# The last layer of an attention and expert kernel: blocks of 512 tokens, and each hidden chunk added at once to the running sums of its block

## The chip, the cores and the metric

The kernel runs on one core of one Trainium2 chip. The metric is the device time of one launch, in microseconds (us): the median over the runs shown. The core has five engines that work side by side, each in the order of its own queue: TensorE (PE, matrix products and transposes), VectorE (DVE), ScalarE (ACT), GpSimd (POOL) and SyncE (SP, which here only issues transfers).

## The reference

Three stages follow one another. Attention over 4 batches, 8 heads and 576 positions gives 2304 token rows of 512 numbers. A layer of 8 experts follows, two for each token. The last layer, the only one that the change touches, is a dense one:

```python
def _moe2_ref(x, w_in, w_out, alpha):      # x: 2304 x 512
    h = x @ w_in                           # w_in: 512 x 2048
    g = np.maximum(h, 0.0) + alpha * np.minimum(h, 0.0)
    return (g @ w_out).astype(np.float32)  # w_out: 2048 x 512
```

Its input x is, for each token, the weighted sum of two rows that the experts left in memory.

## The kernel before

Precision is kept by splitting every float32 operand into a high part and a remainder (float32r); each product is then three matrix products: high by high, remainder by high, high by remainder. `w_hi` (L170, ACT) and `w_lo` (L173, POOL or DVE) split a weight of 128 x 1024, which `w_load` (L165 or L167, SP) brought into a ring of two raw buffers in `m_v0`. Weights 64 to 71 are w_in, 72 to 79 are w_out. 72 to 74 are split during the experts; 75 to 79 are split in the first block of the last layer, after the chunks f = 1, 3, 5, 7 and 9.

The 2304 tokens are 18 tiles of 128. Before, the last layer goes over 9 blocks of 256 tokens (2 tiles). In each block there are two phases.

- **Up.** For each of 16 chunks f of 128 hidden channels, `mm1` (L197) issues 12 products: the stationary operand is 128 x 128 of w_in, the moving one 256 tokens of x, the result one tile of `psum_t` (three buffers). DVE takes it out in two steps (L944, L945) into `tmp`, ACT writes the high part h (L947), POOL the remainder (L948). The hidden values of the whole block stay in `hh` and `hl`.
- **Down.** For each of the 2 tiles, `mm2` (L215) issues 48 products: stationary 128 hidden channels by 128 tokens, moving 128 x 512 of w_out, all summed in one bank of `psum_s`. ACT then copies the sum to one of two `y_tile` buffers (L966) and SP writes it out (L968).

The next block's input is made meanwhile. `y_load` (L865, POOL) issues two indirect gathers for a tile; `combine` (L872 on ACT, L873 on DVE) makes their weighted sum; `x_split` turns it with four PE transposes (L186), and ACT (L189) and DVE (L190) write the two parts of X. Here y_load stands after the chunks 6 and 10 of the up phase, combine and x_split between the products of the down phase.

Nothing is reordered by a planner: each engine runs its instructions in the order in which the program writes them (`tc.manual_schedule()`), and waits on semaphores where an operand or a buffer is not ready.

Ahead of the last layer, expert blocks of 256 and 384 tokens use the same `mm1` and `mm2`. Behind it stands a loop that is run zero times unless an expert overflows.

Of the kernel before, what the change touches and what calls it, by code (L numbers as in the profile page):

```python
# [5 lines left out]
FR = mybir.dt.float32r  # L6
# [4 lines left out]
OP = mybir.AluOpType  # L11
# [3 lines left out]
HP = H // 2  # L15
# [4 lines left out]
NT = N // 128  # L20
# [13 lines left out]
def emit(tc, qt, kt, v, tau, wg, wn, noise, w1, w2, w_in, w_out, alpha, out):  # L34
# [3 lines left out]
    pe, dve, act, pool, sp = nc.tensor, nc.vector, nc.scalar, nc.gpsimd, nc.sync  # L38

    def f32(ap):  # L40
        return ap.bitcast(FT)

    with (
# [7 lines left out]
        yg = dp.tile([N + E * CAP, DM], FT, name="yg")  # L51
# [4 lines left out]
        def cut(t, o, shape, dt=FT):  # L56
            n = 1
            for d in shape:
                n *= d
            w = n * mybir.dt.size(dt) // 4  # L60
            ap = t[:, o:o + w]
            if dt != t.dtype:
                ap = ap.bitcast(dt)
            if len(shape) == 2:
                ap = ap.rearrange("p (a b) -> p a b", a=shape[0])
            if len(shape) == 3:
                ap = ap.rearrange("p (a b c) -> p a b c", a=shape[0], b=shape[1])
            return ap
# [30 lines left out]
        def psum_s():  # L99
            return pp.tile([128, 2, 512], FT, name="ps_s", tag="s", bufs=2)  # L100

        def psum_t(dt=FT):
            return pp.tile([128, 512], dt, name="ps_t", tag="t", bufs=3)
# [10 lines left out]
        alpha_t = cp.tile([128, F2 // 128], FT, name="alpha_t")  # L114
# [27 lines left out]
        WH, WL = {}, {}  # L142
# [11 lines left out]
        rows = [c0([DM]) for _ in range(2)] + [cut(m_rows, DM * i, [DM]) for i in range(2)]  # L154
        row_tile = Ring(rows)
# [13 lines left out]
        def w_hi(n):  # L169
            act.copy(WH[n], wraw[n])  # L170
# [10 lines left out]
            sp.dma_start(r, xg[e * N + t * 128:e * N + t * 128 + 128])  # L181

        def x_split(src, j, x):
            ps = (psum_v, psum_t, psum_t)[j]()
            for c in range(HP):
                pe.transpose(ps[:, c * 128:c * 128 + 128], src[:, c * 128:c * 128 + 128], ident)  # L186
            pv_ = ps.rearrange("p (c t) -> p c t", c=HP)
            xh = x[0][:, :, j * 128:j * 128 + 128]
            act.copy(xh, pv_)  # L189
            dve.tensor_tensor(x[1][:, :, j * 128:j * 128 + 128], pv_, f32(xh), op=OP.subtract)  # L190

        def mm1(ps, n, wc, x, col):

            k = 0
            for d in range(HP):
                for w, xx in ((WH, 0), (WH, 1), (WL, 0)):
                    pe.matmul(ps[:, :n], w[wc[d]][:, col:col + 128], x[xx][:, d, :n],  # L197
                              start=(k == 0), stop=(k == 11))
                    k += 1
            return ps[:, :n]  # L200

        def psum_1(f):
            return psum_t()
# [6 lines left out]
        def mm2(ps, t, n, fs, nf, wc, hs):  # L210
            for f in fs:
                o = f * n + t * 128
                w, c = wc[f // 2], (f % 2) * 512
                for k, (a, ww) in enumerate(((hs[0], WH), (hs[1], WH), (hs[0], WL))):
                    pe.matmul(ps, a[:, o:o + 128], ww[w][:, c:c + 512],  # L215
                              start=(f == 0 and k == 0), stop=(f == nf - 1 and k == 2))

        y_tile = []
# [428 lines left out]
        for b in range(1, B):  # L647
            o = 20 * b
# [31 lines left out]
        for n in range(W0):  # L680
            i = 66 + 2 * n
# [35 lines left out]
        for i in range(END):  # L717
# [29 lines left out]
            if outs:  # L747
                pv(iv)
                if units[iv][2] == HP - 1 or iv < SOLO:
                    T = group_evac(iv)  # L750
# [23 lines left out]
        tmp_tile = Ring([ct([512]) for _ in range(4)])  # L774
        raw64 = ct([1024])
# [9 lines left out]
        hh = mem.tile([128, 16 * 256], FR, name="m_hh")  # L785
        hl = mem.tile([128, 16 * 256], FR, name="m_gate")
        m_x = mem.tile([128, 3072], FR, name="m_v1")
        X = (cut(m_x, 0, [HP, 384], FR), cut(m_x, 1536, [HP, 384], FR))
# [58 lines left out]
        for n in range(W0, 72):  # L847
            t = 1 + 3 * (n - W0)
# [11 lines left out]
        yrows = {}  # L860

        def y_load(T, src):
            for k in range(2):
                r = row_tile()
                pool.indirect_dma_start(  # L865
                    out=r, out_offset=None, in_=src,
                    in_offset=bass.IndirectOffsetOnAxis(ap=posi[:, T, k:k + 1], axis=0))
                yrows[T, k] = r

        def combine(T):  # L870
            y0, y1 = yrows[T, 0], yrows[T, 1]
            act.activation(y0, y0, AF.Copy, scale=wts[:, T, 0:1])  # L872
            dve.scalar_tensor_tensor(y1, y1, wts[:, T, 1:2], y0, op0=OP.mult, op1=OP.add)  # L873

        near = yg[0:N + E * BLOCK0]
        bt = BLOCK0 // 128
        blocks = [(0, bt), (bt, CAP // 128)]
        HS = (hh, hl)
# [21 lines left out]
        for e in range(E):  # L900
            wc = [8 * e + d for d in range(4)]
            wc2 = [8 * e + 4 + d for d in range(4)]
            for bi, (t0, t1) in enumerate(blocks):
                if (e, bi) == (0, 0):
                    continue
                n = (t1 - t0) * 128
# [13 lines left out]
                for t in range(t1 - t0):  # L920
                    ps = psum_s()[:, 0]
                    for f in range(0, 8, 2):
                        mm2(ps, t, n, [f, f + 1], 8, wc2, HS)
                        if f % 4 == 0 and left and (t > 0 or not last):
                            j = left.pop(0)
# [7 lines left out]
            tick()  # L933


        nb = NT // 2
        tmp_tile.aps += [raw64[:, :512], raw64[:, 512:]]
        for j in range(nb):
            for f in range(16):
                hf, fo = divmod(f, 8)  # L940
                ps = mm1(psum_1(f), 256, [64 + 4 * hf + d for d in range(4)], X, fo * 128)
                tmp = tmp_tile()
                t_, g_ = tmp[:, :256], tmp[:, 256:]
                dve.tensor_scalar(t_, ps, 0.0, alpha_t[:, f:f + 1], op0=OP.min, op1=OP.mult)  # L944
                dve.scalar_tensor_tensor(g_, ps, 0.0, t_, op0=OP.max, op1=OP.add)  # L945
                h = hh[:, f * 256:f * 256 + 256]
                act.copy(h, g_)  # L947
                pool.tensor_tensor(hl[:, f * 256:f * 256 + 256], g_, f32(h), op=OP.subtract)  # L948
                if j == 0 and f in (1, 3, 5, 7, 9):
                    w = 75 + f // 2  # L950
                    w_hi(w)
                    w_lo(w, pool)
                    if w < 78:
                        w_load(w + 2)
                if j + 1 < nb and f in (6, 10):
                    y_load(2 * j + 2 + (f - 6) // 4, yg[:, :])
            for t in range(2):
                ps = psum_s()[:, 0]
                if j + 1 < nb:
                    combine(2 * j + 2 + t)  # L960
                mm2(ps, t, 256, range(6), 16, [72 + c for c in range(8)], HS)
                if j + 1 < nb:
                    x_split(yrows[2 * j + 2 + t, 1], t, X)
                mm2(ps, t, 256, range(6, 16), 16, [72 + c for c in range(8)], HS)
                y = y_tile[0]()
                act.copy(y, ps)  # L966
                r = (2 * j + t) * 128
                sp.dma_start(out[r:r + 128], y)  # L968

# [35 lines left out]
        with tc.For_i(0, rv, 1) as it:  # L1007
# [5 lines left out]
            for e in range(E):  # L1013
                ph = up(gx, [8 * e + d for d in range(4)])
                h = []
                for f in range(2):
                    g = gt()
# [12 lines left out]
            for hf in range(2):  # L1030
                ph = up(gx, [64 + 4 * hf + d for d in range(4)])
                for f in range(2):
                    g, h, t_ = gt(), gt(), gt()
                    act.copy(g, ph[:, f])
                    ps = turn(g)
                    for c in range(4):
                        a = 8 * hf + 4 * f + c
                        o = slice(c * 128, c * 128 + 128)
                        dve.tensor_scalar(t_[:, o], ps[:, o], 0.0, alpha_t[:, a:a + 1], op0=OP.min, op1=OP.mult)
                        dve.scalar_tensor_tensor(h[:, o], ps[:, o], 0.0, t_[:, o], op0=OP.max, op1=OP.add)  # L1040
                    for c in range(2):
                        n = 4 * hf + 2 * f + c
# [35 lines left out]
```

## Time and profile before

| what | us |
|---|---|
| median of 3 runs | 1221.8 |
| the runs | 1216.07, 1222.15, 1221.8 |
| the profiled execution, its own time | 1216.61 |
| its span, first to last instruction | 1214.8 |
| last layer: first product to end of the last product's time on the chain | 792.01 to 1203.34 |
| TensorE busy in the span | 1177.5 (97%) |
| VectorE, ScalarE, GpSimd busy | 603.6, 548.9, 519.8 |

The span is what the profile shows of one execution; its own time is 1.8 us longer. Two of the three runs are some 6 us above the third and above the profiled one. Times of rows are counted from the span's start.

### The profile page before, as it was taken

Reading aid. Unit: us, or ns where it says so; the run is one execution under the profiler, and the core shown is the slowest. Engines: PE = TensorE matmul, PEld = TensorE weight load, DVE = VectorE, ACT = ScalarE, POOL = GpSimd, SP = SyncE. Lnnn points to the kernel's source line nnn. Section 1 sums busy time; section 2 is a strip of 40 time slices with the busy share of each in tenths; the row PEclk is TensorE's granted clock in tenths of the full one; section 3 lists DMA queues with packets and bytes.
Section 4 is the critical chain, followed back from the end, with each engine's and each line's share of the span. In section 5 each row is a group of like instructions: output and inputs, shape, how many; then the busy total and the mean of one; then the engine's idle time right before and its main releaser. Section 6 shows DMA issues by size and latency. Waiting matters only on the chain.

```text
span 1214.8 us, 21729 instructions
## 1 busy us (share of the span) xinstructions
PE 1177.5 (97%) x8422; PEld 1046.1 (86%) x8422; DVE 603.6 (50%) x1413; ACT 548.9 (45%) x1109; POOL 519.8 (43%) x617
## 2 busy tenths in 40 slices
PE   7999989999889999999999999999999999999996
PEld 6887777877778989898989898998898898898895
DVE  7968888699534334334445333453352352352340
ACT  7977878778424444444444444441221221221220
POOL 6735545443234444435444444473351351351330
PEclk9999999999999999999999999999999999999998
DMA  7423222232235654556555555521110110110100
GB/s 216 127 83 128 77 91 79 88 114 88 105 147 165 208 191 160 172 205 201 181 175 167 204 183 187 186 96 36 44 44 18 45 44 19 44 45 18 44 10 19
DMA packets 60603, 135.27 MB, mean 111 GB/s; under 512 B 9680, under 2 KB 10320, under 8 KB 60496
## 3 DMA queue, kind: packets, MB, share of 16 engines
q1 hardware_dynamic: 54448, 114.61, 28.5%
q0 software_dynamic: 5760, 18.88, 4.6%
q8 instruction: 68, 1.11, 0.4%
q14 instruction: 39, 0.32, 0.1%
q10 hardware_dynamic: 288, 0.34, 0.1%
HBM read 93.96 MB, written 39.85 MB: 110 GB/s over the span
## 4 chain that ended last, share of the span: by engine, by line
PE 89%; DVE 6%; ACT 2%; issue 1%; DMA 1%; POOL 1%; DVEq 0%; POOLq 0%; ACTq 0%
PE ps_t L197 35%; PE ps_s L215 34%; PE ps_s L347 5%; PE ps_v L441 4%; PE ps_t L399 4%; DVE m_tmp L358 2%; DVE m_hh L382 2%; PE ps_t L186 1%; PE ps_v L429 1%; PE ps_v L432 1%; PE ps_v L186 1%; PE ps_s L197 1%; DVE m_gate L483 1%; PE ps_t L481 1%; PE ps_t L401 1%
## 5 line engine op out<-in xcount | busy, mean ns | idle before, releaser
L215 PE MATMUL ps_s<-m_pair,m_hh 128*128 128x512 f32 x1032 | 338.4, 395 | 0.0
L197 PE MATMUL ps_t<-m_v,m_pair 128*128 128x256 f32 (+1 forms) x2016 | 290.4, 295 | 0.0
L197 PEld LDWEIGHTS ps_t<-m_v,m_pair 128*128 128x128 f32 x2016 | 275.8, 191 | 1.2 <-DVE m_v L190 0.3
L215 PEld LDWEIGHTS ps_s<-m_pair,m_hh 128*128 128x128 f32 x1032 | 193.9, 188 | 39.9
L948 POOL TENSOR_TENSOR m_gate<-m_tmp,m_hh 128x256 fp32r<-128x256 f32 x144 | 104.9, 741 | 249.3 <-ACT m_hh L947 248.3
L215 PE MATMUL ps_s<-m_pair,m_gate 128*128 128x512 f32 x516 | 201.6, 391 | 0.0
L173 POOL TENSOR_TENSOR m_pair<-m_v,m_pair 128x1024 fp32r<-128x1024 f32 x55 | 134.9, 2454 | 138.0 <-ACT m_pair L170 128.9
L197 PE MATMUL ps_t<-m_v,m_early 128*128 128x256 f32 (+1 forms) x1152 | 174.8, 296 | 1.3 <-ACT m_v L189 0.8
L197 PEld LDWEIGHTS ps_t<-m_v,m_early 128*128 128x128 f32 x1152 | 161.8, 191 | 3.0 <-ACT m_v L189 1.1
L208 DVE SCALAR_TENSOR_TENSOR m_gate<-ps_t,m_hh 128x384 fp32r<-128x384 f32 (+1 forms) x120 | 58.4, 493 | 157.9 <-ACT m_hh L207 157.8
L382 DVE SCALAR_TENSOR_TENSOR m_hh<-m_tmp,sm,m_hh 128x576 f32<-128x576 f32 x144 | 129.7, 933 | 1.4 <-ACT sm L363 1.4
L944 DVE TENSOR_SCALAR m_tmp<-ps_t,alpha_t 128x256 f32<-128x256 f32 x144 | 69.7, 484 | 116.6 <-PE ps_t L197 116.1
L947 ACT CAST m_hh<-m_tmp 128x256 fp32r<-128x256 f32 x144 | 58.1, 406 | 144.7 <-DVE m_tmp L945 144.5
L358 DVE TENSOR_SCALAR_CACHE_REDUCE m_tmp<-ps_s 128x576 f32<-128x576 f32 x144 | 103.6, 752 | 24.5 <-PE ps_s L347 22.4
L215 PEld LDWEIGHTS ps_s<-m_pair,m_gate 128*128 128x128 f32 x516 | 97.1, 188 | 18.1
L369 ACT ACTIVATE m_hh<-m_tmp,sm 128x576 f32<-128x576 f32 x144 | 105.8, 783 | 11.2 <-DVE m_tmp L358 11.2
L347 PE MATMUL ps_s<-m_pair 64*128 64x288 f32 (+1 forms) x864 | 95.2, 320 | 11.2 <-DVE m_tmp L358 6.6
L207 ACT ACTIVATE m_hh<-ps_t 128x384 fp32r<-128x384 f32 (+1 forms) x120 | 52.3, 440 | 98.1 <-PE ps_t L197 96.9
L347 PEld LDWEIGHTS ps_s<-m_pair 64*128 64x128 f32 (+1 forms) x864 | 72.7, 193 | 25.6 <-DVE m_tmp L358 11.8
L399 PE MATMUL ps_t<-ident,m_hh 128*128 128x128 f32 x576 | 81.2, 280 | 2.4 <-ACT m_last L411 1.1
L299 POOL TENSOR_TENSOR m_pair<-m_early,m_pair 128x288 fp32r<-128x288 f32 (+1 forms) x60 | 59.2, 1007 | 41.8 <-ACT m_pair L289 28.6
L399 PEld LDWEIGHTS ps_t<-ident,m_hh 128*128 128x128 f32 x576 | 63.6, 141 | 12.7 <-issue 4.7
(200 smaller groups left out, 1443.9 us busy)
## 6 DMA issues: line engine op xcount, KB each, us to landing
m_v<-in_w_dram SPq DMA_DIRECT2D x64, 512.0 KB, 4.0
yg<-m_tmp SPq DMA_DIRECT2D x40, 256.0 KB, 3.4
m_tmp<-in_w_in_dram SPq DMA_DIRECT2D x16, 512.0 KB, 5.3
m_tmp<-in_w_out_dram SPq DMA_DIRECT2D x16, 512.0 KB, 5.0
m_v<-xg SPq DMA_DIRECT2D x20, 256.0 KB, 5.6
m_rows<-xg SPq DMA_DIRECT2D x20, 256.0 KB, 4.5
m_early<-in_kt_dram SPq DMA_DIRECT2D x15, 320.0 KB, 3.3
yg<-m_gate SPq DMA_DIRECT2D x18, 256.0 KB, 2.0
```

The lines of the kernel that those rows point to most:

```text
L173: eng.tensor_tensor(WL[n], wraw.pop(n), f32(WH[n]), op=OP.subtract)
L197: pe.matmul(ps[:, :n], w[wc[d]][:, col:col + 128], x[xx][:, d, :n], start=(k == 0), stop=(k == 11))
L208: dve.scalar_tensor_tensor(hs[1][:, f * n:f * n + n], ps, 0.0, f32(h), op0=OP.max, op1=OP.subtract)
L215: pe.matmul(ps, a[:, o:o + 128], ww[w][:, c:c + 512], start=(f == 0 and k == 0), stop=(f == nf - 1 and k == 2))
L299: pool.tensor_tensor(lo[:, c], raw[:, c], f32(hi[:, c]), op=OP.subtract)
L347: pe.matmul(u["ps", h][:, x, :288], lhs, kk[r, o:o + 288], start=(k == 0), stop=(k == 2))
L358: dve.tensor_scalar(u["sp"][:, h].rearrange("p (a b) -> p a b", a=2), ps[:, :, :288], -0.125, None, op0=OP.mult, op1=OP.min, accum_out=u[" ...
L369: act.activation(u["em"][:, h], u["sp"][:, h], AF.Exp, bias=u["sm"][:, h:h + 1], scale=-1.0)
L382: dve.scalar_tensor_tensor(u["em"][:, h], u["sp"][:, h], sm[:, 2 + h:3 + h], u["em"][:, h], op0=OP.is_le, op1=OP.mult, accum_out=acc)
L399: pe.transpose(ps[:, j * 128:j * 128 + 128], emf[:, o + j * 128:o + j * 128 + 128], ident)
L944: dve.tensor_scalar(t_, ps, 0.0, alpha_t[:, f:f + 1], op0=OP.min, op1=OP.mult)
L948: pool.tensor_tensor(hl[:, f * 256:f * 256 + 256], g_, f32(h), op=OP.subtract)
```

## The change

The last layer is cut into one block of 256 tokens and four of 512 (`sizes`). Each chunk f of 128 hidden channels now has an up part (`up_chunk`, 12 products with 256 or 512 moving columns) and a down part (`down_chunk`), in which its three products for each of the block's tiles are added at once to running sums, one bank of `psum_s` for each tile; a block of 512 tokens holds all four banks from its first chunk to its last. The down part of a chunk is issued two chunks after its up part, across the borders of blocks too. The hidden values are kept for few chunks only (`small`, four buffers; `large`, five, three of them in the memory of the raw weights and two where `small` was). X has three places that take turns. The gathers, the sum and the transposes of the next block's tiles are spread over the chunks (`next_x`): in the first block y_load follows chunk 4, 6, 8 or 10, in the others chunk 2, 5, 8 or 11; combine comes two chunks and x_split three chunks after y_load. The gathers' ring is now the two buffers of `m_rows` and two halves of `raw64`. VectorE's two steps work in place in one 512-wide buffer of a ring of four (before: two 256-wide halves, ring of six). After the last chunk of a block, its two or four sums are copied out one behind the other through the two `y_tile` buffers.

```diff
@@ -181,7 +181,7 @@
             sp.dma_start(r, xg[e * N + t * 128:e * N + t * 128 + 128])
 
         def x_split(src, j, x):
-            ps = (psum_v, psum_t, psum_t)[j]()
+            ps = (psum_v, psum_t, psum_t, psum_t)[j]()
             for c in range(HP):
                 pe.transpose(ps[:, c * 128:c * 128 + 128], src[:, c * 128:c * 128 + 128], ident)
             pv_ = ps.rearrange("p (c t) -> p c t", c=HP)
@@ -933,39 +933,77 @@
             tick()
 
 
-        nb = NT // 2
-        tmp_tile.aps += [raw64[:, :512], raw64[:, 512:]]
-        for j in range(nb):
-            for f in range(16):
-                hf, fo = divmod(f, 8)
-                ps = mm1(psum_1(f), 256, [64 + 4 * hf + d for d in range(4)], X, fo * 128)
-                tmp = tmp_tile()
-                t_, g_ = tmp[:, :256], tmp[:, 256:]
-                dve.tensor_scalar(t_, ps, 0.0, alpha_t[:, f:f + 1], op0=OP.min, op1=OP.mult)
-                dve.scalar_tensor_tensor(g_, ps, 0.0, t_, op0=OP.max, op1=OP.add)
-                h = hh[:, f * 256:f * 256 + 256]
-                act.copy(h, g_)
-                pool.tensor_tensor(hl[:, f * 256:f * 256 + 256], g_, f32(h), op=OP.subtract)
+
+
+        sizes = [bt] + [4] * ((NT - bt) // 4)
+        XS = [X, (cut(hh, 0, [HP, 512], FR), cut(hh, 2048, [HP, 512], FR)),
+              (cut(m_x, 0, [HP, 512], FR), cut(hl, 0, [HP, 512], FR))]
+        small = Ring([cut(hl, 2048 + 512 * i, [512], FR) for i in range(4)])
+        large = Ring([])
+        row_tile.aps = rows[2:] + [raw64[:, :512], raw64[:, 512:]]
+        hid, acc = {}, {}
+
+        def up_chunk(j, f):
+            n = 128 * sizes[j]
+            hf, fo = divmod(f, 8)
+            ps = mm1(psum_t(), n, [64 + 4 * hf + d for d in range(4)], XS[j if j < 2 else 2 - j % 2], fo * 128)
+            g = tmp_tile()[:, :n]
+            dve.tensor_scalar(g, ps, 0.0, alpha_t[:, f:f + 1], op0=OP.min, op1=OP.mult)
+            dve.scalar_tensor_tensor(g, ps, 0.0, g, op0=OP.max, op1=OP.add)
+            h = (small if j == 0 else large)()
+            hid[j, f] = h[:, :n], h[:, n:2 * n]
+            act.copy(h[:, :n], g)
+            pool.tensor_tensor(h[:, n:2 * n], g, f32(h[:, :n]), op=OP.subtract)
+
+        def down_chunk(j, f):
+            if f == 0:
+                a = [psum_s() for _ in range(sizes[j] // 2)]
+                acc[j] = [a[t // 2][:, t % 2] for t in range(sizes[j])]
+            h = hid.pop((j, f))
+            w, c = 72 + f // 2, (f % 2) * 512
+            for t in range(sizes[j]):
+                ps = acc[j][t]
+                for k, (x, ww) in enumerate(((0, WH), (1, WH), (0, WL))):
+                    pe.matmul(ps, h[x][:, t * 128:t * 128 + 128], ww[w][:, c:c + 512],
+                              start=(f == 0 and k == 0), stop=(f == 15 and k == 2))
+                if f == 15:
+                    y = y_tile[0]()
+                    act.copy(y, ps)
+                    r = (sum(sizes[:j]) + t) * 128
+                    sp.dma_start(out[r:r + 128], y)
+
+        def next_x(j, f):
+
+            if j + 1 == len(sizes):
+                return
+            T, x = sum(sizes[:j + 1]), XS[j + 1 if j < 1 else 2 - (j + 1) % 2]
+            for t in range(4):
+                o = 4 + 2 * t if j == 0 else 2 + 3 * t
+                if f == o:
+                    y_load(T + t, yg[:, :])
+                if f == o + 2:
+                    combine(T + t)
+                if f == o + 3:
+                    x_split(yrows.pop((T + t, 1)), t, x)
+
+        chunks = [(j, f) for j in range(len(sizes)) for f in range(16)]
+        for i in range(len(chunks) + 2):
+            if i < len(chunks):
+                j, f = chunks[i]
+                if (j, f) == (1, 0):
+                    m_v0 = mem.tile([128, 3072], FR, name="m_v0")
+                    large.aps = ([cut(m_v0, 1024 * i, [1024], FR) for i in range(3)]
+                                 + [cut(hl, 2048 + 1024 * i, [1024], FR) for i in range(2)])
+                up_chunk(j, f)
                 if j == 0 and f in (1, 3, 5, 7, 9):
                     w = 75 + f // 2
                     w_hi(w)
                     w_lo(w, pool)
                     if w < 78:
                         w_load(w + 2)
-                if j + 1 < nb and f in (6, 10):
-                    y_load(2 * j + 2 + (f - 6) // 4, yg[:, :])
-            for t in range(2):
-                ps = psum_s()[:, 0]
-                if j + 1 < nb:
-                    combine(2 * j + 2 + t)
-                mm2(ps, t, 256, range(6), 16, [72 + c for c in range(8)], HS)
-                if j + 1 < nb:
-                    x_split(yrows[2 * j + 2 + t, 1], t, X)
-                mm2(ps, t, 256, range(6, 16), 16, [72 + c for c in range(8)], HS)
-                y = y_tile[0]()
-                act.copy(y, ps)
-                r = (2 * j + t) * 128
-                sp.dma_start(out[r:r + 128], y)
+                next_x(j, f)
+            if i >= 2:
+                down_chunk(*chunks[i - 2])
 
 
 
```

## Rows read from the trace of the kernel before

**Rows 1.** The page: busy time of each engine.

```profile
PE 1177.5 (97%) x8422; PEld 1046.1 (86%) x8422; DVE 603.6 (50%) x1413; ACT 548.9 (45%) x1109; POOL 519.8 (43%) x617
```

**Rows 2.** Chain that ended last, last layer: start us, us, what.

```profile
792.01 23.03 PE ps_t L197 x192
815.05 4.11 PE ps_s L215 x18
819.16 0.44 PE ps_v L186 x4
819.59 10.95 PE ps_s L215 x48
830.54 0.44 PE ps_t L186 x4
830.98 6.85 PE ps_s L215 x30
837.83 23.03 PE ps_t L197 x192
...
1181.54 21.80 PE ps_s L215 x96
1203.34 0.03 ACTq L966
1203.37 0.04 issue
1203.41 0.59 ACT m_tmp L966
```

**Rows 3.** Busy time by stretch: first up phase, first down phase.

```profile
core 0: us, PE busy (x) PEld busy (x) DVE busy (x) ACT busy (x) POOL busy (x), PEclk, DMA share, GB/s
792.00:815.00 23.00, 23.00 (x194) 23.00 (x193) 13.63 (x30) 10.92 (x21) 18.69 (x17) 1.00 0.34 109
815.00:837.80 22.80, 22.80 (x107) 18.83 (x106) 4.28 (x6) 3.52 (x7) 8.57 (x9) 1.00 0.11 35
```

**Rows 4.** The same chain, experts: blocks of 256 and of 384 tokens.

```profile
675.73 11.51 PE ps_t L197 x96
...
699.63 16.66 PE ps_t L197 x96
```

**Rows 5.** Groups by line, last layer, shapes apart: busy us, mean ns, idle before.

```profile
L948 POOL TENSOR_TENSOR m_gate<-m_tmp,m_hh 128x256 fp32r<-128x256 f32 x144 | 104.9, 741 | 249.3 <-ACT m_hh L947 248.3 <-DVEq L1007 0.7
...
L944 DVE TENSOR_SCALAR m_tmp<-ps_t,alpha_t 128x256 f32<-128x256 f32 x144 | 69.7, 484 | 116.6 <-PE ps_t L197 116.1 <-issue 0.4
L945 DVE SCALAR_TENSOR_TENSOR m_tmp<-ps_t,m_tmp 128x256 f32<-128x256 f32 x144 | 61.2, 425 | 15.5 <-POOL m_gate L948 0.9
L947 ACT CAST m_hh<-m_tmp 128x256 fp32r<-128x256 f32 x144 | 58.1, 406 | 144.7 <-DVE m_tmp L945 144.5
...
L173 POOL TENSOR_TENSOR m_pair<-m_v,m_pair 128x1024 fp32r<-128x1024 f32 x4 | 9.7, 2413 | 0.2 <-ACT m_pair L170 0.2
...
L872 ACT ACTIVATE m_rows<-m_rows,wts 128x512 f32<-128x512 f32 x8 | 5.8, 726 | 0.0
...
L190 DVE TENSOR_TENSOR m_v<-ps_t,m_v 128x512 fp32r<-128x512 f32 x8 | 5.5, 692 | 25.2 <-ACT m_v L189 25.2
...
L170 ACT CAST m_pair<-m_v 128x1024 fp32r<-128x1024 f32 x4 | 4.2, 1047 | 3.3 <-DMA m_v<-wf_out 3.3
```

**Rows 6.** Timeline, first chunk of the last layer and weight 75.

```profile
793.56 0.48 DVE L944 TENSOR_SCALAR m_tmp<-ps_t,alpha_t 128x256 f32<-128x256 f32 x1 [4.13 <-PE ps_t L197]
...
795.02 0.74 POOL L948 TENSOR_TENSOR m_gate<-m_tmp,m_hh 128x256 fp32r<-128x256 f32 x1 [15.30 <-ACT m_hh L947]
...
797.34 2.40 POOL L173 TENSOR_TENSOR m_pair<-m_v,m_pair 128x1024 fp32r<-128x1024 f32 x1 [0.21 <-ACT m_pair L170]
```

**Rows 7.** Timeline, late in the experts: gathers and the combine behind them.

```profile
772.52 1.01 POOL L865 DMA_INDIRECT m_v<-yg,posi  x1 [0.15 <-issue]
...
773.83 0.96 POOL L865 DMA_INDIRECT m_v<-yg,posi  x1 [0.30 <-issue]
...
776.89 0.73 ACT L872 ACTIVATE m_v<-m_v,wts 128x512 f32<-128x512 f32 x1 [0.76 <-DMA m_v<-yg,posi]
777.31 2.41 POOL L173 TENSOR_TENSOR m_pair<-m_v,m_pair 128x1024 fp32r<-128x1024 f32 x1
...
777.65 2.63 DVE L873 SCALAR_TENSOR_TENSOR m_v<-m_v,wts 128x512 f32<-128x512 f32 x1 [1.86 <-DMA m_v<-yg,posi]
```

**Rows 8.** Line 873, the combine's second step: ns min/median/max.

```profile
L873 DVE SCALAR_TENSOR_TENSOR m_rows<-m_rows,wts x9: 740/752/754, 781.3 to 1148.5; 128x512 f32<-128x512 f32 x9
```

**Rows 9.** Line 968, the output's transfers.

```profile
DMA to landing us min/median/max: 2.0/2.0/2.0
```

## The prediction

> **What bounds the kernel now.** I read the page first: TensorE is busy 97% of the span, the next engine half of it [rows 1]. A busy share alone does not say that nothing else could end last, so I read the chain of work that ended last over the last layer. From 792.01 to 1203.34 it is TensorE alone: an up phase of 23.03 us (192 products), then a down phase in pieces of 4.11, 10.95 and 6.85 us (18, 48 and 30 products) with two groups of transposes of 0.44, nine times over [rows 2]. So a product with 256 moving columns costs 23.03 / 192 = 0.1199 us there, one with 512 costs 10.95 / 48 = 0.228. The table by stretch shows that the other engines have room: in the up phase VectorE is busy 13.6 of 23.0 us, GpSimd 18.7 in the first block, and in the down phase all of them are nearly idle; the granted clock is 1.00 [rows 3]. So in this layer time can be won only by cheaper or fewer TensorE instructions, and lost wherever TensorE is made to wait.
>
> **The price of a product by its width.** The experts' blocks give two more points on the same line 197: 96 products of 256 columns took 11.51 us, 96 of 384 took 16.66 [rows 4], or 0.1199 and 0.1735 each. Each 128 columns more cost 0.0536, so 512 would cost 0.2271 by the straight line and 0.228 by the down products [rows 2]. All three points leave a fixed share of about 0.012 us per product, whatever its width. That share is what a wider block saves.
>
> **What the change removes.** Eight blocks of 256 become four of 512. Two up phases before: 2 x 23.03 = 46.06. One up phase of 192 products at 0.228: 43.78. Saved 2.28 each, 9.1 in all; with 0.2271 it would be 9.8. The lower bound, no fixed share saved (512 columns at 2 x 0.1199), is 0. I take 9.1, since line 215 has measured 512 columns with the same operand types. The down products stay 864 with the same shapes, and the transposes 64: no change.
>
> [...]
>
> **Borders.** Up and down now alternate chunk by chunk, some 160 borders instead of 17, and each chunk brings waits for an evacuated bank or for h. The first piece after a border, 18 products in 4.11 us, is 0.2283 each against 0.2281 in the long piece; the up phase with its 16 chunk starts runs evenly [rows 2]. So a border whose wait is already met costs nothing I can see; the upper bound is the rounding, 0.01 us each, 1.4 in all.
>
> **Are the waits met? Blocks of 512.** From the end of an up part to its down part lie two down parts (12 x 0.228 = 2.74) and two up parts (2.74), 10.9 us. The hidden values need: L944 at 512 wide about 0.75 (0.484 and 256 more elements at the pace at which lines 945 and 190, VectorE's 0.425 for 256 and 0.692 for 512, differ), L945 0.69, ACT about 0.62 (between 0.406 for 256 and 1.047 for 1024), GpSimd about 1.29 (between 0.741 and 2.413) [rows 5]; some 3.6 with the gaps. Covered threefold; doubling each 256 price gives 4.2, also covered. In the last two chunks there are no up parts ahead, 5.5 us remain, still enough. GpSimd gets 1.29 of work per 5.5 us, and two gathers every third chunk.
>
> The path with least room is the next tile's: combine waits in ACT's queue behind this chunk's h, its second step on VectorE behind GpSimd's subtraction, and the transposes stand in TensorE's own queue after the next up part, 5.48 us on. By the prices above h is done at 2.2, the first combine step at 3.0, and the second at 3.8, or 4.3 if it waits for GpSimd. About a microsecond to spare: no stall. The gather has two chunks, 11 us, to land.
>
> **The first block.** Here a chunk lasts only 12 x 0.1199 + 6 x 0.228 = 2.81, and GpSimd still splits weights 75 to 79. Behind the gathers stand, in GpSimd's queue, the next remainders of h and w_lo; behind combine, in ACT's queue, the next h. I lay GpSimd's queue out by hand from 792.01. Chunk f's up part ends at 796.33 + 2.81 (f - 2). As in the first chunk before, h's remainder could start 1.6 us after the up part [rows 6], but each w_lo takes 2.41 [rows 5]. So w_lo(76), behind chunk 3, runs 801.7 to 804.1, the remainder of chunk 4 to 804.85, and the first two gathers start at 805.0 and 806.3 (1.3 apart, as in the trace [rows 7]). In the trace the first gather was waited for until 4.4 us after its start and the second until 3.8 [rows 7]: data at 809.4 and 810.1. ACT's combine step takes 0.73, to 810.1. VectorE's takes 0.75 [rows 8], but 2.63 where w_lo ran beside it: it ended 0.56 after that w_lo did [rows 7]. Beside w_lo(77), which ends at 810.35, it ends between 810.9 and 811.6. The transposes are due when chunk 7's up part ends, at 810.4. TensorE waits 0.5 to 1.3 us, I take 1.0.
>
> The same done for the other three tiles, with what the wait has moved: GpSimd still has 2 x 0.74 + 2.41 + 2.5 = 6.4 us of work per 5.6 us pair of chunks until w_lo(79), so the second wait is about 0.85, the third 0.5, the fourth 0.1. Sum 2.5 us. Bounds: nothing, if the gathers land in 3 us; 5, if each of the first three comes 1 us later still beside the weight transfers. Weights are in time: down chunk 6, the first that needs weight 75, starts at 813.2, and 75 is split by 799.7 already before [rows 6].
>
> **The end.** Before, the last copy starts at 1203.41, when TensorE is done, and takes 0.59 [rows 2]; its transfer lands 2.0 later [rows 9]. Now four sums end 0.68 apart and share two buffers. Let the first be ready at T. Its copy ends at T + 0.6 and its transfer lands at T + 2.65; the second lands at T + 3.35. The third copy waits for the first landing and ends at T + 3.3, the fourth ends at T + 3.95. TensorE is done at T + 2.05: the last copy ends 1.9 us after it instead of 0.6. Cost 1.3; if the transfers also slow one another, 2.2. I take 1.4, near the first. Between blocks the same row of copies costs nothing: the next down part starts 2.74 later and needs the third bank another 1.4 later.
>
> **The sum.** 9.1 saved, 2.5 lost in the first block, 1.4 at the end: 5.2 us less. Against the profiled execution's own time, 1216.6 (the span and 1.8 around it): 1211.4. That execution lies 5.2 below the median of the runs; the four times known (1216.1, 1216.6, 1221.8, 1222.2) have a mean of 1219.2, and less 5.2 that is **1214**, which I predict for the median. A change within 0.5% (6.1 us) is what a measurement of this kernel can't tell from none.
>
> **Rivals.**
> - *The wide product saves nothing.* If the fixed share were tied to line 197's operands and 512 columns cost 2 x 0.1199, the up parts would gain 0 and the waits remain: 3.9 more, 1220.5 by own time. Against it: three widths lie on one straight line, and the one of 384 is line 197 itself [rows 4]. [...] Chance 0.1.
> - *The first block stops TensorE for longer (slower).* One mechanism: the transposes stand in TensorE's queue behind rows that GpSimd's queue sends for too late. For it: GpSimd has more work there than time, and 2.63 us for a 0.75 us step [rows 7]. From 7.7 us of waiting in the four places together (1.9 each) the gain is gone; at 3.5 each it is 14, and the time 1222.9. Against it: it takes gathers of some 6 us, the trace has 3.8 to 4.4. Chance 0.1, half of it slower beyond what can be told.
> - *The first block costs next to nothing.* With gathers of 3 us and a combine that slips in ahead of w_lo, only the end is lost: 7.7 less, 1208.9. Chance 0.15.
> - *Borders cost.* 0.04 us each would be 6, and the gain gone: 1217. Against it the even pieces in [rows 2]. Chance 0.05.
>
> My forecast keeps 0.6.
>
> **How the numbers follow.** The forecast's own range is 3 to 7 us less. The runs part by 6 us among themselves, so a median of few may stand at either edge: the range runs from 1208 (the lower pair less 8) to 1221 (the rival without gain on the lower pair, or the forecast on the upper pair with its dearest stalls). Faster by over 0.5% takes the rival with a free first block, the upper part of the forecast, and the case that the two medians fall on different edges in its favour: 0.46. Within 0.5%: the lower part of the forecast, most of the no-gain rival and the borders: 0.46. Slower: 0.08.
>
> **What would show it.** In the changed kernel's chain, up parts of 512 should take 2.74 us for 12 products and down parts the same; 2.88 for the up parts would mean the first rival. TensorE's idle time should lie before the transposes of the first block's chunks 7, 9, 11 and 13, 2 to 3 us together, put down to VectorE's line of combine, and nowhere in the blocks of 512. TensorE should be done about 6.6 us earlier than before, at 1196.7, and the last copy should start about 1.3 us after that. The prediction would be wrong if stalls show at the borders, or if a transpose waits in the later blocks.

## The result, and the profile after

The changed kernel takes 1234.2 us (median of 4 runs, 1230.9 to 1235.3) beside 1219.8 for the kernel before (4 runs): a ratio of 1.0118, interval 1.0094 to 1.0143. It is slower by 1.2%; forecast were 1214 and a range to 1221. The profiled execution took 1234.9 by its own time, 1233.2 by its span.

The page of the changed kernel, part 1 and the granted clock in 40 slices:

```profile
PE 1181.0 (96%) x7654; PEld 1012.4 (82%) x7654; DVE 585.6 (47%) x1285; ACT 535.1 (43%) x1045; POOL 511.3 (41%) x553
...
PEclk9999999999999999999999999999998998998998
```

TensorE has 768 products fewer than in [rows 1], and yet is busy longer, and its granted clock (PEclk, in tenths of full speed), 9 in every slice but the last before, now dips near the end. Who let it wait in the last layer is in the table of waits (engine, line, who released it: us in total, times, longest):

```profile
PE ps_s L967 <- ACT m_tmp L971: 12.8, 9, 2.2
PE ps_v L186 <- DVE m_rows L873: 1.1, 1, 1.1
PE ps_t L186 <- DVE m_tmp L873: 0.5, 2, 0.3
PE ps_t L186 <- DVE m_rows L873: 0.3, 1, 0.3
```

The last three lines are the forecast waits of the first block's transposes, 1.9 us. The first is not in the prediction: down products that wait for the copies of the sums. The chain that ended last shows one such place, from the second block to the third:

```profile
929.57 2.72 PE ps_t L197 x12
932.29 2.72 PE ps_s L967 x12
935.01 2.73 PE ps_t L197 x12
...
939.95 0.59 ACT m_tmp L971
940.54 0.04 issue
940.58 2.18 PE ps_s L967 x6
...
942.83 0.59 ACT m_tmp L971
943.43 0.04 issue
943.47 1.65 PE ps_s L967 x3
945.12 4.31 PE ps_t L197 x12
949.42 2.72 PE ps_s L967 x12
```

Away from the border, an up part and a down part take 2.72 us each, 0.2267 a product: a little less than forecast from [rows 2, 4]. At the border the chain leaves TensorE twice for a copy, and the up part behind it takes 4.31 for the same twelve products. The timeline tells what each waited for (L967 are the down products, L955 the high part, L971 the copies; in brackets how long the engine had stood idle and who ended it):

```profile
937.57 0.84 PE L967 MATMUL ps_s<-m_last,m_v 128*128 128x512 f32 x3
...
939.43 0.62 ACT L955 CAST m_v<-m_tmp 128x512 fp32r<-128x512 f32 x1 [4.84 <-DVE m_tmp L952]
939.95 0.58 ACT L971 COPY m_tmp<-ps_s 128x512 f32<-128x512 f32 x1
...
940.58 2.17 PE L967 MATMUL ps_s<-m_last,m_v 128*128 128x512 f32 x6 [2.17 <-ACT m_tmp L971]
941.58 0.59 ACT L971 COPY m_tmp<-ps_s 128x512 f32<-128x512 f32 x1 [1.05 <-PE ps_s L967]
942.83 0.59 ACT L971 COPY m_tmp<-ps_s 128x512 f32<-128x512 f32 x1 [0.66 <-PE ps_s L967]
943.47 1.65 PE L967 MATMUL ps_s<-m_last,m_v 128*128 128x512 f32 x3 [0.72 <-ACT m_tmp L971]
```

The first tile's three products are over at 938.4. Its copy starts only at 939.95, because ScalarE's queue first has the high part (L955) of the up part that has just ended. The second tile's products start when the copy is done. The third tile's run on; the fourth's wait again, for the third's copy. So products wait where the second bank of a pair follows a copy of the first: the two sums of one `psum_s` tile. And the table by stretch (us, TensorE's busy us and instructions, granted clock, share and GB/s of the transfers) shows what the wait brings after it:

```profile
935.00:938.00 3.00, 3.00 (x15) 1.00 0.00 0
938.00:940.50 2.50, 0.41 (x2) 1.00 0.00 0
940.50:943.50 3.00, 2.20 (x7) 0.67 0.38 149
943.50:948.40 4.90, 4.90 (x12) 0.51 0.32 123
948.40:951.00 2.60, 2.60 (x13) 1.00 0.00 0
```

Behind the idle time the clock is granted at 0.51, its 1.2 GHz level, until 948.4. The up parts behind the four borders between blocks take 4.06, 4.31, 4.53 and 4.64 us instead of 2.72.

### The profile page after: what moved, and what is told of

Same layout as the page of the kernel before. It is cut to its first block, busy times and chain, and to the rows that moved or that the text cites. A ratio compares the mean times of both kernels' runs of the same rounds, so it can differ in the third digit from the quotient of the medians.

```text
span 1233.2 us, 19851 instructions
## 1 busy us (share of the span) xinstructions
PE 1181.0 (96%) x7654; PEld 1012.4 (82%) x7654; DVE 585.6 (47%) x1285; ACT 535.1 (43%) x1045; POOL 511.3 (41%) x553
## 3 DMA queue, kind: packets, MB, share of 16 engines
q8 instruction: 62, 1.02, 0.3%
## 4 chain that ended last, share of the span: by engine, by line
PE 82%; DVE 7%; issue 3%; ACT 3%; DMA 2%; POOL 2%; SPq 0%; ACTq 0%; DVEq 0%; POOLq 0%
PE ps_t L197 31%; PE ps_s L215 16%; PE ps_s L967 15%; PE ps_s L347 5%; PE ps_v L441 4%; PE ps_t L399 4%; DVE m_tmp L358 2%; DVE m_hh L382 2%; PE ps_t L186 1%; PE ps_v L429 1%; PE ps_v L432 1%; POOL m_early L173 1%; PE ps_s L197 1%; PE ps_v L186 1%; DVE m_gate L483 1%
## 5 line engine op out<-in xcount | busy, mean ns | idle before, releaser
L197 PE MATMUL ps_t<-m_v,m_pair 128*128 128x384 f32 (+2 forms) x1216 | 220.9, 318 | 0.2
L197 PEld LDWEIGHTS ps_t<-m_v,m_pair 128*128 128x128 f32 x1216 | 187.2, 190 | 8.8 <-DVE m_gate L208 0.4
L215 PE MATMUL ps_s<-m_pair,m_hh 128*128 128x512 f32 x528 | 175.6, 396 | 0.0
L951 DVE TENSOR_SCALAR m_tmp<-ps_t,alpha_t 128x512 f32<-128x512 f32 (+1 forms) x80 | 55.8, 697 | 241.1 <-PE ps_t L197 240.9
L197 PE MATMUL ps_t<-m_v,m_early 128*128 128x256 f32 (+2 forms) x672 | 130.0, 325 | 1.3 <-ACT m_v L189 0.8
L956 POOL TENSOR_TENSOR m_v<-m_tmp,m_v 128x512 fp32r<-128x512 f32 x39 | 50.4, 1293 | 159.1 <-ACT m_v L955 159.1
L215 PEld LDWEIGHTS ps_s<-m_pair,m_hh 128*128 128x128 f32 x528 | 99.2, 188 | 20.4
L197 PEld LDWEIGHTS ps_t<-m_v,m_early 128*128 128x128 f32 x672 | 107.6, 192 | 7.2 <-ACT m_v L189 1.1
L955 ACT CAST m_v<-m_tmp 128x512 fp32r<-128x512 f32 x39 | 24.2, 621 | 182.1 <-DVE m_tmp L952 182.1
L956 POOL TENSOR_TENSOR m_gate<-m_tmp,m_gate 128x512 fp32r<-128x512 f32 (+1 forms) x41 | 44.2, 1077 | 130.0 <-ACT m_gate L955 125.8
L967 PE MATMUL ps_s<-m_pair,m_v 128*128 128x512 f32 x396 | 96.0, 391 | 0.0
L967 PE MATMUL ps_s<-m_pair,m_gate 128*128 128x512 f32 x360 | 89.2, 393 | 0.0
L955 ACT CAST m_gate<-m_tmp 128x512 fp32r<-128x512 f32 (+1 forms) x41 | 22.0, 537 | 150.0 <-DVE m_tmp L952 148.6
```

The lines of the kernel that those rows point to most:

```text
L215: pe.matmul(ps, a[:, o:o + 128], ww[w][:, c:c + 512], start=(f == 0 and k == 0), stop=(f == nf - 1 and k == 2))
L951: dve.tensor_scalar(g, ps, 0.0, alpha_t[:, f:f + 1], op0=OP.min, op1=OP.mult)
L956: pool.tensor_tensor(h[:, n:2 * n], g, f32(h[:, :n]), op=OP.subtract)
L967: pe.matmul(ps, h[x][:, t * 128:t * 128 + 128], ww[w][:, c:c + 512], start=(f == 0 and k == 0), stop=(f == 15 and k == 2))
```

## The experiments

One number serves to compare profiles, since the work ahead of the last layer starts it between 787.8 and 794.7 from one execution to another: the layer's length, from the start of its first product to the end of its last. Ratios are of medians to the kernel before on the same chip, with their intervals.

| kernel | layer, us | TensorE's waits on copies | ratio |
|---|---|---|---|
| before | 411.5 | none | 1 |
| changed | 429.1 | 12.8 | 1.0118 (1.0094 to 1.0143) |
| late copies | 403.8 | none | 0.9935 (0.9915 to 0.9955) |
| no bank wait | 403.8 | none | 0.9935 (0.9915 to 0.9954) |
| filled wait | 420.8 | 0.2 | 1.0065 (1.0048 to 1.0081) |
| narrow, late copies | 422.1 | none | 1.0093 (1.0059 to 1.0126) |
| four outputs | 425.7 | 12.0 | 1.0114 (1.0095 to 1.0132) |
| down first | 429.3 | 12.6 | 1.0140 (1.0114 to 1.0166) |
| copy first | 414.0 | 7.5 | 1.0021 (1.0009 to 1.0034) |
| early gather | 402.5 | none | 0.9915 (0.9896 to 0.9933) |
| early gather, again | 402.6 | none | 0.9940 (0.9919 to 0.9961) |
| all mended | 402.6 | none | 0.9932 (0.9914 to 0.9950) |
| all mended, again | 402.4 | none | 0.9928 (0.9911 to 0.9944) |

**Late copies.** The products of a block's last chunk first, then its copies.

```diff
-                if f == 15:
-                    y = y_tile[0]()
-                    act.copy(y, ps)
-                    ...
+            for t in range(sizes[j] if f == 15 else 0):
+                y = y_tile[0]()
+                act.copy(y, acc[j][t])
+                r = (sum(sizes[:j]) + t) * 128
+                sp.dma_start(out[r:r + 128], y)
```

> The changed kernel, but the last chunk of a block issues all its products first and its two or four copies behind them. Theory (TensorE's queue holds a wait for the copy of the first bank before the products of the second bank of the same psum tile, and the clock falls behind that wait): the 12.8 us of waits on the copies and the half-clock products behind them are gone, 402.2 us of products and some 2.5 of the first block's waits remain, TensorE is done near 1197, the fourth copy ends 3.9 later; about 1213 by own time, 20 to 23 below the changed kernel and 3 or so below the kernel before. Rival (the banks themselves hold the next block up, however the copies are placed): the wait moves to the next block's first products, 1228 or more.

Measured: 1211.3, beside 1218.0 for the kernel before. The waits on copies are gone and did not come back at the next block's first products, so the rival falls. In its chain, over the same border, every part takes 2.72:

```profile
927.96 2.72 PE ps_s L967 x12
930.68 2.72 PE ps_t L197 x12
933.40 2.72 PE ps_s L967 x12
936.12 2.72 PE ps_t L197 x12
938.84 2.72 PE ps_s L967 x12
```

**No bank wait.** The order of the changed kernel, copies in their old places; the wait alone is declared needless.

```diff
+                    if f == 15 and t % 2:
+                        tc.declare_no_dep(m.ins, copied.ins, reason="other bank")
...
-                    act.copy(y, ps)
+                    copied = act.copy(y, ps)
```

> The changed kernel with the order of all instructions kept; only the waits are left out by which products of an odd tile wait for the copy of the even tile, which lies in another bank. Theory (the wait is one that the program puts there for the whole psum tile, not one that the banks need): the same gain as late copies, and one or two us more, because the copies start earlier: about 1212. Rival (a product that writes one bank while ScalarE reads the other of the pair is itself slow): 1225 to 1235, with stretched products in the last chunks.

Measured: 1211.2, the layer as long as with late copies, the clock at 1.00 at every border, so the wait was one of the program. At a border the copy and the products that waited for it do not even meet. With no wait all twelve products run through from 935.23, the second tile's three from about 935.9 to 936.6, and the copies, behind the high part, start only at 937.61. At the kernel's end, where no high part stands ahead, they do meet:

```profile
1194.87 2.88 PE L967 MATMUL ps_s<-m_last,m_gate 128*128 128x512 f32 x12
1195.75 1.27 ACT L973 COPY m_tmp<-ps_s 128x512 f32<-128x512 f32 x2 [3.84 <-PE ps_s L967]
```

These twelve products take 2.88 by their records, as the twelve from 935.23 do, with the clock at 1.00. So a copy out of one bank and products into the other go side by side at full pace. That is how the Trainium skill has it ("PSUM — Partial Sum Buffer", "Summary: rules for kernel authors"): to read while products run, use another bank, and guard by bank. TensorE's queue in the last chunk, from its second product on, written out from the program, shows the difference (row, line, instruction, what it waits for, count). The changed kernel:

```
2797 L967 MATMUL ps_s<-m_last,m_gate 128x512 [waits Pool_49]
2798 L967 MATMUL ps_s<-m_last,m_gate 128x512
2799 L967 MATMUL ps_s<-m_last,m_gate 128x512 [waits Activation_49]
2800 L967 MATMUL ps_s<-m_last,m_gate 128x512 x5
2801 L967 MATMUL ps_s<-m_last,m_gate 128x512 [waits Activation_49]
2802 L967 MATMUL ps_s<-m_last,m_gate 128x512 x2
```

No bank wait has, in place of the last five, one row of ten products without a wait.

**Filled wait.** Idle products ahead of the waiting ones, into a bank that nobody reads.

```diff
+                if f == 15 and t % 2:
+                    spare = psum_v()
+                    for _ in range(10 if t == 1 else 4):
+                        pe.matmul(spare, h[0][:, 0:128], WH[w][:, c:c + 512], start=True, stop=True)
```

> The changed kernel with idle products of 512 columns into a spare bank ahead of the waiting ones in a block's last chunk: 10 before the second tile, 4 before the fourth (2.3 and 0.9 us). Their results go nowhere. TensorE still comes late to the products, but is not idle before them. Theory (about half the loss is half clock behind the idle wait): no product behind the wait is stretched, the four borders cost 3.2 us each and not 6.4, about 1226 (1223 to 1230). Rival (the clock falls for the pattern of the products or for the transfers, not for the idle time): stretched products stay, 1234 or more.

Measured: 1227.0. The timeline at the same border (L969 are the idle products):

```profile
936.80 2.43 PE L969 MATMUL ps_v<-m_last,m_v 128*128 128x512 f32 x10
...
939.14 1.66 PE L971 MATMUL ps_s<-m_last,m_v 128*128 128x512 f32 x6
...
940.63 1.07 PE L969 MATMUL ps_v<-m_last,m_v 128*128 128x512 f32 x4
...
941.85 0.97 PE L971 MATMUL ps_s<-m_last,m_v 128*128 128x512 f32 x3
```

Six products take 1.66 here and 2.17 in the changed kernel, three 0.97 and 1.65; the granted clock is 1.00 throughout. The products that matter come no earlier (939.1, 3.0 after the down part's start at 936.1; in the changed kernel 3.0 after 937.6). The layer is 8.3 shorter than the changed kernel's, though 66 products of 0.2267, 15.0 us, were added. The waiting products and the transfers are the same, and with the idle time filled the clock falls at none of the four borders. So the fall takes the idle time. It does not always follow it: one border in four outputs and one in down first, shown there, kept 1.00 behind the same wait.

**Narrow, late copies.** Nine blocks of 256, chunk by chunk.

```diff
-        sizes = [bt] + [4] * ((NT - bt) // 4)
+        sizes = [bt] * (NT // bt)
...
-            for t in range(4):
-                o = 4 + 2 * t if j == 0 else 2 + 3 * t
+            for t in range(2):
+                o = 4 + 4 * t
```

> The chunk-wise order of the changed kernel with late copies, but all nine blocks of 256 tokens as before the change. Theory (the width alone brings the 9.1 us; borders cost nothing): no fixed share is saved, the product time is that of the kernel before, the first block's waits stay: 1 to 3 us slower than the kernel before, about 1219 by own time. Rival (up and down in turn cost at each border): 5 us slower or more, with products of uneven pace at the borders.

Measured: 1230.4, 12 slower than before instead of the 1 to 3 that I expected. The waits name why:

```profile
PE ps_v L186 <- DVE m_rows L873: 3.2, 8, 1.1
PE ps_t L186 <- DVE m_tmp L873: 2.3, 8, 0.7
```

Of the 10.6 by which the layer is longer than before, 5.5 are these waits and some 3.5 the transposes behind them (0.66 instead of 0.44, 16 times). All 16 sets of transposes wait for their sum, not the first block's alone: with chunks of 2.8 us, one chunk between combine and transposes is too short in every block. I had seen that for the first block and forgotten it here. The borders themselves cost little: in its chain an up part takes 1.43 and a down part 1.39, 2.82 a chunk where [rows 2] give 2.81, some 1.4 over 144 chunks. So the time is the rival's (5 or more), but not its cause; the first theory holds in its main part (no width, no gain), and the expectation missed a term of the kind that the prediction had.

**Four outputs.** Two more buffers for the copies, from the second block on.

```diff
+                if (j, f) == (1, 8):
+                    y_tile[0].aps = y_tile[0].aps + tmp_tile.aps[2:]
+                    tmp_tile.aps = tmp_tile.aps[:2]
```

> The changed kernel with four output buffers from the second block on (two of the four evacuation buffers are given to the copies), so that no copy waits for an output transfer to land; copies and waits between products stay where they are. Theory (TensorE waits for the copies themselves, and for ScalarE's earlier work ahead of them; the transfers add little): the second wait of a border falls from 0.7 to 1.0 to about 0.7, 1 to 2 us in all, the clock still falls: 1231 to 1234 by own time. Rival (the two buffers and the 2.0 us landing are the main cost): 1226 or less.

Measured: 1232.5; waits on copies 12.0 instead of 12.8. The output transfers' landing is a small part. The layer is 3.4 shorter all the same, because at the fourth border the clock did not fall (1.00 from 1126 to 1142), behind a wait as long as the others:

```profile
1130.39 1.65 PE L967 MATMUL ps_s<-m_last,m_v 128*128 128x512 f32 x6 [2.17 <-ACT m_tmp L971]
1132.71 0.97 PE L967 MATMUL ps_s<-m_last,m_v 128*128 128x512 f32 x3 [0.68 <-ACT m_tmp L971]
```

From this down part's start to the next one's it takes 8.9 (1127.4 to 1136.3), the changed kernel's fourth border 11.9 (1128.1 to 1140.0), of which 0.35 is a longer second wait. That leaves 2.6 for the half clock. What made this border different, no run here shows.

**Down first.** The down part two chunks back ahead of the up part of the step.

```diff
+            if i >= 2:
+                down_chunk(*chunks[i - 2])
             if i < len(chunks):
...
-            if i >= 2:
-                down_chunk(*chunks[i - 2])
```

> The changed kernel with the down part of two chunks back issued ahead of the up part of this chunk in each step, so that in ScalarE's queue the copies no longer stand behind a high part that waits for the up part just issued. Theory (2.2 us of each border's first wait is mostly that queue, the copy itself is 0.6): the first wait falls to about 0.7, the sum of the waits on copies from 12.8 to 6 or 7; the time falls by 6 at least, to 1229, and by up to 16 if the clock stays up after two waits of 0.7. Rival (the 2.2 us are the copy and its semaphores): the waits stay at 12 or more, 1233.

Measured: 1235.4, waits on copies 12.6, and two new ones, 1.1 in sum, for GpSimd's remainder. By its expectation that would speak for the rival; but the edit did not do what it was meant for. The parts still alternate, so the copies stand behind the high part of another, equally fresh, up part. The next run does it properly. Here too one border, the first, kept the clock at 1.00:

```profile
845.23 0.96 PE L967 MATMUL ps_s<-m_last,m_gate 128*128 128x512 f32 x3 [2.10 <-ACT m_tmp L971]
```

It takes 6.5 from one down part to the next (842.3 to 848.8), the changed kernel's first border, with the same wait, 8.1 (845.9 to 854.0): 1.6 for the half clock.

**Copy first.** The high part and the remainder go behind the copies, in the steps where there are copies.

```diff
+            def split():
+                act.copy(h[:, :n], g)
+                pool.tensor_tensor(h[:, n:2 * n], g, f32(h[:, :n]), op=OP.subtract)
+            return split
...
+                split = up_chunk(j, f)
+                if i < 2 or chunks[i - 2][1] < 15:
+                    split()
...
                 down_chunk(*chunks[i - 2])
+                if i < len(chunks) and chunks[i - 2][1] == 15:
+                    split()
```

> The changed kernel, but where a block's copies fall, the high part and the remainder of the up part just issued go into the queues of ScalarE and GpSimd behind the copies and not ahead of them. (Down first, meant for this, only moved the copies behind the high part of another chunk.) Theory (of the first wait's 2.2 us, 1.5 is the high part ahead of the copy in ScalarE's queue): the first wait of a border falls to about 0.7; the second grows to 1.2, since the third copy now waits longer for the first transfer; 8 us of waits instead of 12.8, and a time 5 or more below the changed kernel, 1229 or less, the clock's part open. Rival (2.2 us is what copy and semaphores take): 12 us or more of waits, 1233.

Measured: 1216.3 beside 1213.2 for the kernel before on that chip, 0.2% above it where the changed kernel is 1.2% above. The waits at a border:

```profile
932.34 1.66 PE L971 MATMUL ps_s<-m_last,m_v 128*128 128x512 f32 x6 [0.68 <-ACT m_tmp L975]
...
935.05 0.96 PE L971 MATMUL ps_s<-m_last,m_v 128*128 128x512 f32 x3 [1.05 <-ACT m_tmp L975]
935.85 0.39 PE L197 MATMUL ps_t<-m_v,m_early 128*128 128x512 f32 x1
```

0.68 for the copy itself, so 1.5 of the 2.2 was the high part ahead of it; 1.05 where the third copy waits for the first transfer. And nothing is stretched: the clock stays at 1.00 behind these waits. The theory had left that part of the gain open.

**Early gather**, on top of no bank wait.

```diff
-        row_tile.aps = rows[2:] + [raw64[:, :512], raw64[:, 512:]]
+        row_tile.aps = rows + [raw64[:, :512], raw64[:, 512:]]
...
-                o = 4 + 2 * t if j == 0 else 2 + 3 * t
+                o = 2 + 2 * t if j == 0 else 2 + 3 * t
...
-                if f == o + 3:
+                if f == o + (5 if j == 0 else 3):
...
+                    row_tile.aps = row_tile.aps[2:]
                     m_v0 = mem.tile([128, 3072], FR, name="m_v0")
```

> No bank wait, and in the first block the gathers stand two chunks earlier (chunks 2, 4, 6 and 8) with a ring of six row buffers, so that the sum has a chunk more and the transposes come where they were. Theory (the transposes of the first block wait for the sum, 1.9 us in four places and some refilling): these waits are gone, 2 to 3 us less than no bank wait, about 1209. Rival (GpSimd's queue is the bound there, and earlier gathers only push the remainders of h back): as long as no bank wait, with waits for GpSimd at the down products.

**All mended**: early gather, no bank wait and four outputs.

> No bank wait, early gathers and four output buffers together. Theory (the terms add): the end's third copy no longer waits for a transfer, some 2.7 us less than early gather, 1205 to 1207 by own time, 1.0% below the kernel before. Rival (the terms hide one another): no better than early gather.

Measured on one chip: 1209.8 and 1210.6. The transposes' waits are gone; one wait for GpSimd's remainder, of 0.3 and 0.4, has come in their place, and the layer is 1.3 shorter than with no bank wait, not 2 to 3. All mended is no faster than early gather, which is the rival, not the 1205 to 1207 expected. The two were run once more together:

> Early gather once more, beside all mended on one chip: 1208 to 1210 by the median.

> All mended once more. Its last copy came 0.6 us behind the last product, with two output buffers 3.3; if the terms add, its median lies 1.5 to 2.7 us below early again, if the runs' spread hides it, within 1.

Measured: 1204.9 and 1204.5, beside 1213.2 for the kernel before on that chip, where it was 1219.1 on the other. Four outputs end the last copy 0.6 after the last product, where early gather's ends 2.0 after it, and not 3.3 as the expectation has it. From the last product to the end of the span that is 11.8 and 12.0 instead of 12.4 and 12.6, no more than the spread of the runs hides. In the second run of all mended one set of transposes waited again, 1.0, for VectorE's step on the set before (L190).

## Why the prediction was wrong

The step that failed is the one on the end of a block. It said that TensorE is done at T + 2.05, and that between blocks the row of copies costs nothing. Both took the copies for work behind TensorE, with only the next block's banks to free. In the program the copy of a sum is written between its products and those of the next tile, and two sums share one `psum_s` tile. So TensorE's queue holds a wait for the copy of the first bank before the products of the second: nine times, 12.8 us, and 25.3 with what follows from them. The kernel before used one bank of each such tile only, so its trace could not show it; the listing of the change could, had I followed each copy to who waits for it. What each wait costs I could have had from my own steps: the copy stands in ScalarE's queue behind a high part that is done 2.2 us after its up part, which is my own figure.

The layer is 25.3 longer than with late copies. 12.8 are the waits themselves. Copy first has nine waits too, 7.5 us in sum, is 10.2 longer than late copies and its clock does not fall: some 2.7 for starting up again nine times. The remainder, 9.8, is the half clock. The mean clock of the four borders (0.86 over 12 us, 0.74 over 13 twice, 0.76 over 14) makes 3.4 us at half clock at the first and some 6.7 at each of the others, 23.6 in all, of which half is lost where TensorE is busy: 11.8 at most. Filled wait, which only keeps TensorE busy, gets 8.3 back in spite of 15.0 us of added products. The two borders that kept 1.00 put a price on it: 1.6 at the first border (down first) and 2.6 at the fourth (four outputs). With 2.6 for the second and third as well that is 9.4, near the remainder. The 2.7 is an estimate from copy first alone.

The other terms, read from late copies and no bank wait:

- **Width**, 9.1 forecast. An up part of 192 products takes 16 x 2.72 = 43.5 instead of 43.8, so 2.54 saved per block and 10.2 in all. The straight line through [rows 4] was the better estimate, and the fixed share is saved.
- **Down products and borders**, 0 forecast. 12 products in 2.72 against 0.228 each: about 1.0 saved over the 768 of the wide blocks. The borders cost little: in late copies it is 89.03 from one set of transposes to the same set a block on (955.16 to 1044.19), where 32 parts of 2.72 and four sets of 0.44 make 88.8, so 0.2 a block and some 0.9 in all.
- **First block**, 2.5 forecast: waits of 1.1, 0.2 to 0.3, 0.3 and 0.3, 1.9 in sum, at chunks 7, 9, 11 and 13 and put down to line 873 as the prediction said, and transposes of 0.63 to 0.66 instead of 0.44 behind them, 0.8 in sum. The timeline at the first of them:

```profile
805.29 0.96 POOL L865 DMA_INDIRECT m_rows<-yg,posi  x1
...
808.22 2.41 POOL L173 TENSOR_TENSOR m_pair<-m_v,m_pair 128x1024 fp32r<-128x1024 f32 x1
809.49 0.72 ACT L872 ACTIVATE m_rows<-m_rows,wts 128x512 f32<-128x512 f32 x1
810.24 1.62 DVE L873 SCALAR_TENSOR_TENSOR m_rows<-m_rows,wts 128x512 f32<-128x512 f32 x1 [1.18 <-ACT m_rows L872]
...
811.92 0.66 PE L186 MATMUL ps_v<-ident,m_rows 128*128 128x128 f32 x4 [1.09 <-DVE m_rows L873]
```

  Each time is within 0.5 of the one laid out by hand: gather 805.0, data by 809.4, sum at 811.6 at the latest (805.29, 809.49 and 811.86 here). VectorE's step took 1.62 beside w_lo where [rows 8] have 0.75. No step of the four sums waited for a gather, so the slower rival, which takes gathers of some 6 us, is not what happened, though its sign was right. In the blocks of 512 no transposes waited, as forecast.
- **The end**, 1.4 forecast. From the last product's end to the end of the span, 11.46 before, 12.35 with late copies and 12.64 with no bank wait: 0.9 and 1.2.

In the layer these make 10.2 and 1.0 saved, 0.9, 1.9 and 0.8 lost, 7.6 us less; it is 7.7 shorter with late copies.

With the wait taken away, no bank wait is 0.65% below the kernel before, and the forecast of 5.2 less would have been 0.43%. The mechanism of the gain was right; the price of the copies was put at nothing.

## What to carry to other kernels

A buffer that is one tile to the program is one thing to wait for, however many banks it spans: write all products of the pair before the first copy (late copies), declare the wait needless (no bank wait), or give each sum a tile of its own (not run here). When a kernel moves a copy from behind a phase into it, follow it in both directions: what stands ahead of it in its engine's queue, and which later instruction waits for it. A wait of TensorE may cost twice its length, since the products behind it can run at half clock; small idle products, or shorter waits, kept the clock here.

## What the runs showed of the hardware

In the changed kernel the granted clock fell from 1.00 to about 0.5 (2.4 to 1.2 GHz) after TensorE had stood idle for 2.1 to 2.2 us, behind all four borders between blocks, and came back 3.4 us later at the first and 6.8 at the others. It does not fall each time: of four such borders in four outputs and four in down first, one each stayed at 1.00, behind 2.17 and 2.10. Behind waits of up to 1.1 us (the first block's transposes, both waits of a border in copy first, 0.68 and 1.02 at the end of the changed kernel) it stayed at 1.00. So it did in the kernel before, ahead of the experts, behind waits of 1.66 and 1.43 (L401, at 163 and 320 us); behind one of 2.12 (L565, at 336) it fell for 3.4 us there too. The price of a product in this kernel is linear in its columns from 256 to 512: 0.1199, 0.1735 and 0.2267 us.
